# Attention with chosen chunks and a gated MLP: w_in products split for three batches, x^T copied by VectorE, a new order on every engine

## The chip, the cores and the metric

The kernel runs on one core of a Trainium2 chip. The metric is the device time of one execution in microseconds. The core's engines are named as the profile names them: PE (TensorE, with PEld for its weight loads), DVE (VectorE), ACT (ScalarE), POOL (GpSimd) and SP (SyncE, which here only issues DMAs).

## The reference

Two stages follow each other. The first is attention over 4 batches, 8 heads, 768 positions and head size 64, in which each query sees only the 6 chunks (of 32 keys) that an upper bound of its scores ranks highest. The second is a gated MLP over the result.

```python
# attention: k in 24 chunks of 32 keys
k_min, k_max = k_chunks.min(axis=3), k_chunks.max(axis=3)
ub = np.sum(np.maximum(q * k_min, q * k_max), axis=-1)      # for each query and chunk
ub = np.where(causal, ub, -1e9)
top_chunks = np.argsort(ub, axis=-1)[..., -6:]
scores = np.where(sel & causal_positions, scale * q @ k.T, -1e9)
attn = softmax(scores)
x = (attn @ v)                                              # (4, 768, 512)
# gated MLP
h = gelu_tanh(x @ w_in)                                     # (4, 768, 1024)
u, v = h[..., :512], h[..., 512:]
v_n = (v - mean) / sqrt(var + 1e-6) * g_ln
v_s = einsum('ts,bsd->btd', w_sg, v_n) + b_sg[None, :, None]
out = x + (u * v_s) @ w_out
```

## The kernel before

The work is cut into 16 **pairs** of heads (pair p holds heads 2p and 2p+1) and 4 **batches** (batch b is made of pairs 4b to 4b+3). Everything is written down as a list of operations in `_build`. Each has an engine, a function that issues its instructions, and the names of what it reads and writes; `link` turns these into semaphore waits. The order is not the order of that list. `TABLE` holds, for each engine, the numbers of its operations in the order in which it issues them, and in `slots` the PSUM slot of every tile; `place` follows it. Each engine issues strictly in its order, so an operation that waits holds up all that stand behind it on the same engine, and SP's list is one queue for nearly all DMAs.

For each pair: two loads each of k rows and q rows and one or two of v rows (`load_rows` L527, `load_v` L536 and L542, into three buffers each); fp32 transposes on PE (L549); minimum and maximum of each chunk on DVE (L577) and their difference (L596); copies of the transposed k and q out of PSUM on ACT or DVE (`evac`, L449 for ACT and L452 for DVE); the positive part of q (L615 on ACT, L618 on DVE) and a cast of q on POOL (L624); the upper bounds on PE (L659 for pairs 0 to 3, L706 for two pairs at once after that); then on DVE transposes of the bounds (L669, L715), the 8 largest of each (L676, L726), a comparison (L682, L731) and the transpose of the mask (L686, L734). From pair 4 on, DMAs bring the mask (L739), the copy of k (L590) and constant rows (L593, L751) into the operands of the scores, so that one matmul gives score and mask. The scores (L833 and L839, or L794) go through the exponential on ACT (L848, or L800), POOL zeroes the part above the diagonal (L857, L805), and PE multiplies with v (L878, and L884 on the diagonal). DVE divides by the sum (L894, L896) and writes x into `XS`.

For each batch, x must be transposed for the product with w_in. Its four quarters dk = 0 to 3 belong to the four pairs. In batch 0 all four are transposed on PE (`xtrans`, L918) and copied out of PSUM. In batches 1 to 3 the first three are transposed by a DMA (L905) and only the last on PE. The constant `XEV` names the engine of that copy, batch by batch.

`moe_h` computes h: six tiles of 128 rows for the half that is normalized (L942, then the gelu on ACT, L947, and statistics on DVE, L951), and eight tiles for u (L961, gelu L967). Each tile is a sum of four matmuls over dk. For b < `HSPL` a tile is two operations, one over dk = 0 to 2 and one over dk = 3, and its PSUM tile may lie in any of four slots; otherwise it is one operation, and in batches 0 to 2 its tile lies in slots 2 or 3:

```python
cut = NDK - 1 if b < HSPL else 0
t = ps_g.tile((2, 3) if not cut and b < B - 1 else None)
for x, (k0, k1) in enumerate(((0, cut), (cut, NDK)) if cut else ((0, NDK),)):
```

`moe_g` follows: the normalized half (L995, after a power on POOL, L983) times w_sg (L1013), scaled and shifted on DVE (L1030), times u (L1034), times w_out (L1046), plus x (L1055, into `osb` or `vgb`), stored by L1062. The weights come by DMA (L441) into buffers that are free at the start, and POOL casts them (L445); w_sg is also transposed on PE (L495). Gelu and the exponential need different tables on ACT, so ACT runs all gelus of a batch in one go, with a table load before and after.

Of the kernel before, what the change touches and what calls it, by code (L numbers as in the profile page):

```python
# [10 lines left out]
F32 = mybir.dt.float32  # L11
# [249 lines left out]
def _build(nc, ctx, q, k, v, w_in, g_ln, w_sg, b_sg, w_out, out):  # L261
# [4 lines left out]
    NT = S // 128  # L266
# [22 lines left out]
    def T(name, shape, dt):  # L289
        return ctx.enter_context(nc.sbuf_tensor(name, list(shape), dt))  # L290
# [18 lines left out]
    NQS = 3  # L309
    NBULK = 0  # L310
# [15 lines left out]
    HSPL = 1  # L326
# [18 lines left out]
    XEV = ("act","act","act","act")  # L345
    qn = [T(f"qn{i}", [128, NT, 2, DH], F32) for i in range(NQS)]
    kn = [T(f"kn{i}", [128, NT, 2, DH], F32) for i in range(NQS)]
# [174 lines left out]
    def load_rows(p, nm, src, dst):  # L522
        s = p % NQS
        for h0, h1 in ((0, 1), (1, 2)) if p < SPLIT else ((0, 2),):
            for i in range(2):
                j0, j1 = 3 * h0, 3 * h1
                P.op("act" if i == 1 and p < BOTH else "sp", lambda e, i=i, j0=j0, j1=j1: e.dma_start(  # L527
                    dst[s][:, j0:j1, i, :], bass.AP(src.tensor, (2 * p + i) * S * DH + 128 * DH * j0,
                                                    [[DH, 128], [128 * DH, j1 - j0], [1, DH]])), dmac(),
                     (nm, p, i, h0), writes=[(nm, s, h, i) for h in range(h0, h1)], dma=f"{nm}{s}_{i}{h0}",  # L530
                     xfer=XROW * (h1 - h0) / 2, bulk=NBULK)

# [21 lines left out]
    def kside(p):  # L554
        s, w = p % NQS, p % NW
# [555 lines left out]
    for p in range(4, NP + 4):  # L1111
# [39 lines left out]
    "act": (  # L1151
# [11 lines left out]
    "dve": (  # L1163
# [18 lines left out]
    "pool": (  # L1182
# [80 lines left out]
```

## Time and profile before

| what | value |
|---|---|
| median of 3 runs | 218.98 us (217.86 to 219.22) |
| the profiled execution, time | 216.24 us |
| the profiled execution, span | 214.4 us |
| granted TensorE clock in it | 0.998 |
| PE busy | 202.5 us, 94% of the span |
| DVE busy | 184.2 us, 86% |
| ACT busy | 162.0 us, 76% |
| POOL busy | 89.0 us, 41% |
| DMA, packets' time as a share of 16 engines' span, the largest queue | 72.3% |

A row of a timeline or of the chain has the start in us from the span's start, the length in us, the engine, the line, and what is written from what; in brackets behind it stands how long the engine had been idle and what ended that. A row of the groups has busy time and mean nanoseconds of one instruction behind the bar, then the idle time before them. A row for one line has least, median and greatest duration in ns.

| stretch, us from the span's start | what PE mostly does there |
|---|---|
| 0 to 44.7 | pairs 0 to 3: transposes, bounds, scores, values |
| 44.7 to 58 | w_in products of batch 0 |
| 58 to 98.8 | w_sg and w_out of batch 0, attention of pairs 4 to 7 |
| 98.8 to 113 | w_in products of batch 1 |
| 113 to 152.5 | w_sg and w_out of batch 1, attention of pairs 8 to 12 and most of 13 |
| 152.5 to 165 | w_in products of batch 2 |
| 165 to 184.9 | w_sg and w_out of batch 2, the rest of the attention |
| 184.9 to 214.4 | batch 3's MLP and the last stores |

### The profile page before, as it was taken

To read this page: it belongs to the slowest core of one execution; us is meant where nothing else is said; L and a number is where in the kernel's file an instruction comes from. 1 tells how busy PE (TensorE), PEld (TensorE's weight loads), DVE (VectorE), ACT (ScalarE), POOL (GpSimd) and SP (SyncE) were. 2 spreads that over 40 slices of the span, in tenths; PEclk is the share of its full clock that TensorE was granted. 3 is DMA by queue.
4 is the path that set the end of the run, shared out by engine and by line. 5 is a ranking of instruction groups with operands and counts; after the bars stand their busy time and mean duration, and the time that the engine had idled before them with its cause. 6 is when DMAs were issued, how large, how long until landed. Compare 5 with 4: busy or idle time off the path is not lost.

```text
span 214.4 us, 5903 instructions
## 1 busy us (share of the span) xinstructions
PE 202.5 (94%) x2314; PEld 133.7 (62%) x2326; DVE 184.2 (86%) x534; ACT 162.0 (76%) x249; POOL 89.0 (41%) x119
## 2 busy tenths in 40 slices
PE   7979999999999899997999899999999999999993
PEld 3547777745766577785466577679545668555642
DVE  3999999779999999894999798979797876778994
ACT  2468999988599599999769988989967888664000
POOL 8426598993274357634120664565202313002000
PEclk9999999999999999999999999999999999999999
DMA  7999989997999969898998986753721006201207
GB/s 152 219 218 192 280 193 293 343 346 149 223 228 256 178 194 235 183 172 212 243 214 182 204 193 181 180 162 90 68 48 28 3 25 152 46 3 49 98 26 268
DMA packets 91338, 36.06 MB, mean 168 GB/s; under 512 B 84144, under 2 KB 86448, under 8 KB 91312
## 3 DMA queue, kind: packets, MB, share of 16 engines
q1 hardware_dynamic: 91024, 35.31, 72.3%
q8 instruction: 18, 0.29, 0.6%
q10 hardware_dynamic: 288, 0.39, 0.5%
q14 instruction: 8, 0.07, 0.1%
HBM read 24.77 MB, written 6.29 MB: 145 GB/s over the span
## 4 chain that ended last, share of the span: by engine, by line
PE 52%; DVE 21%; ACT 9%; SPq 7%; DMA 6%; issue 2%; DVEq 0%
PE PSG L1013 8%; PE PSG L961 8%; PE PSC L794 7%; PE PSG L942 6%; PE PSG L1046 6%; PE PSG L549 4%; DVE W L577 4%; ACT E L848 4%; PE PSG L878 3%; SPq L527 3%; DVE m L726 2%; PE PSG L706 2%; DVE U L715 2%; DMA out_dram<-osb 2%; ACT E L800 2%
## 5 line engine op out<-in xcount | busy, mean ns | idle before, releaser
L800 ACT ACTIVATE E<-PSC 128x1024 bf16<-128x1024 f32 (+1 forms) x72 | 63.1, 919 | 7.6 <-PE PSC L794 7.3
L794 PE MATMUL PSC<-QA,KA 128*128 128x128 bf16 (+2 forms) x336 | 37.8, 246 | 0.6 <-DMA QA<-Dt 0.5
L577 DVE TENSOR_REDUCE W<-PSG 128x12 f32<-128x384 f32 x64 | 32.4, 546 | 3.7 <-PE PSG L549 3.7
L1013 PE MATMUL PSG<-wsgT,vhat 128*128 128x384 bf16 x192 | 34.9, 326 | 0.0
L624 POOL CAST QA<-qT 64x768 bf16<-64x768 f32 (+1 forms) x28 | 23.9, 857 | 22.9 <-ACT qT L449 16.1
L805 POOL TENSOR_SCALAR_AFFINE_SELECT E<-E 128x768 bf16<-128x768 bf16 x24 | 20.7, 862 | 29.9 <-ACT E L800 29.6
L794 PEld LDWEIGHTS PSC<-QA,KA 128*128 128x128 bf16 x336 | 24.0, 98 | 8.2 <-ACT E L800 1.9
L1013 PEld LDWEIGHTS PSG<-wsgT,vhat 128*128 128x128 bf16 x192 | 17.7, 98 | 11.3 <-DVE uT L1034 0.5
L967 ACT ACTIVATE uT<-PSG 128x384 bf16<-128x384 f32 x32 | 15.5, 490 | 11.7 <-PE PSG L961 11.1
L961 PE MATMUL PSG<-xT,winb 128*128 128x384 bf16 x128 | 23.9, 326 | 0.0
L848 ACT ACTIVATE E<-PSC 128x1024 bf16<-128x1024 f32 (+3 forms) x26 | 21.4, 863 | 2.6 <-PE PSC L839 2.2
L1046 PE MATMUL PSG<-woutb,uT 128*128 128x512 bf16 (+1 forms) x92 | 21.8, 370 | 1.3 <-DMA KA<-INDF 0.5
L1030 DVE SCALAR_TENSOR_TENSOR PSG<-PSG,glnT,bsgbc 128x384 f32<-128x384 f32 x32 | 19.8, 621 | 3.0 <-PE PSG L1013 2.7
L942 PE MATMUL PSG<-winb,xT 128*128 128x512 bf16 x92 | 21.2, 379 | 0.9 <-issue 0.5
L634 POOL CAST vx<-vn 128x768 bf16<-128x768 f32 x16 | 13.3, 833 | 20.3 <-DMA vn<-in_v_dram 16.2
L449 ACT ACTIVATE KA<-PSG 128x384 bf16<-128x384 f32 (+1 forms) x38 | 18.3, 493 | 2.8 <-DVE W L577 2.7
L878 PE MATMUL PSG<-vx,E 128*128 128x65 bf16 x480 | 19.8, 194 | 0.3 <-ACT E L800 0.2
L878 PEld LDWEIGHTS PSG<-vx,E 128*128 128x128 bf16 x480 | 17.4, 98 | 2.7 <-issue 0.7
L1034 DVE TENSOR_TENSOR uT<-PSG,uT 128x384 bf16<-128x384 f32 x32 | 17.7, 554 | 0.8
L896 DVE TENSOR_TENSOR XS<-PSG,rden 128x384 bf16<-128x384 f32 x32 | 17.6, 552 | 0.8
L951 DVE BATCH_NORM_STATS2 stats<-vgb 128x6 f32<-128x512 f32 x24 | 16.1, 687 | 2.2 <-ACT vgb L947 1.9
L961 PEld LDWEIGHTS PSG<-xT,winb 128*128 128x128 bf16 x128 | 11.7, 98 | 9.4 <-ACT uT L967 1.8
(87 smaller groups left out, 332.5 us busy)
## 6 DMA issues: line engine op xcount, KB each, us to landing
kn<-in_k_dram SPq DMA_DIRECT2D x32, 192.0 KB, 4.5
qn<-in_q_dram SPq DMA_DIRECT2D x32, 192.0 KB, 4.4
vn<-in_v_dram SPq DMA_DIRECT2D x12, 384.0 KB, 5.1
out_dram<-osb SPq DMA_DIRECT2D x18, 256.0 KB, 2.3
vn<-in_v_dram SPq DMA_DIRECT2D x8, 192.0 KB, 5.7
uT<-in_moe_w_sg_dram SPq DMA_DIRECT2D x4, 384.0 KB, 5.8
vgb<-in_moe_w_in_dram SPq DMA_DIRECT2D x3, 512.0 KB, 5.3
KA<-INDF SPq DMA_DIRECT2D x12, 96.0 KB, 3.8
```

Source lines behind the costliest of these rows:

```text
L577: P.op("dve", lambda d, m=m, op=op, src=src, h0=h0, h1=h1: d.tensor_reduce(W[w][:, m, 12 * h0:12 * h1].rearrange("p (h c) -> p h c", h=h1 ...
L624: P.op("pool", lambda g, i=i, r0=r0, r1=r1: g.tensor_copy(QA[w][i or 0][r0:r1, :], qT[r][r0:r1, :]), gps(S, 250 if i == 1 else 150), ("qca ...
L794: r = e.matmul(t.ap()[:, o:o + n], KA[w][i][:, 128 * kb:128 * kb + 128], QA[w][i][:, q0:q0 + n], start=True, stop=True)
L800: P.op("act", lambda e, t=t, c0=c0, c1=c1, i=i: e.activation(E[es][:, i, c0:c1], t.ap()[:, 0:c1 - c0], ACTF.Exp, scale=SCALE), act(c1 - c0 ...
L805: P.op("pool", lambda g, ev=ev: g.affine_select(ev, ev, pattern=[[0, NT], [1, 128]], compare_op=ALU.is_ge, fill=0.0, base=0, channel_multi ...
L848: P.op("act", lambda e, t=t, c0=c0, c1=c1, n=n: e.activation(E[es][:, :, c0:c1], t.ap().rearrange("p (i x) -> p i x", i=2)[:, :, 0:n], ACT ...
L878: r = e.matmul(t.ap()[:, 65 * (qb - q0):65 * (qb - q0) + 65], E[es][:, i, at[kb, qb]:at[kb, qb] + 128], vx[w][:, kb, i, :], start=x == 0, ...
L942: r = e.matmul(t.ap()[:, 0:F], xT[s][:, dk, 128 * qt:128 * qt + 128], winb[:, dk, F:DFF], start=(dk == 0), stop=(dk == NDK - 1), skip_grou ...
L961: r = e.matmul(t.ap()[:, 0:TG], winb[:, dk, 128 * fb:128 * fb + 128], xT[s][:, dk, TG * tg:TG * tg + TG], start=(dk == 0), stop=(dk == NDK ...
L1013: r = e.matmul(t.ap()[:, 0:TG], vhat[s][:, sb, 128 * fb:128 * fb + 128], wsgT[:, sb, TG * tg:TG * tg + TG], start=(sb == 0), stop=(sb == N ...
L1030: P.op("dve", lambda d, t=t, fb=fb, tg=tg: d.scalar_tensor_tensor(t.ap()[:, 0:TG], t.ap()[:, 0:TG], glnT[:, fb:fb + 1], bsgbc[:, TG * tg:T ...
L1046: r = e.matmul(t.ap()[:, 0:n1 - n0], gT[s][:, fb, 128 * qt:128 * qt + 128], woutb[:, fb, n0:n1], start=(fb == 0), stop=(fb == NF - 1))
```

## The change

Three constants change what is computed where. `HSPL` goes from 1 to 3: in batches 1 and 2 too, each w_in tile becomes two operations. `XEV` goes to DVE for batches 1 to 3: the copy of the last quarter of x^T leaves ACT. The number of k buffers gets a name of its own, `NKS`, and stays 3. The 28 new operations shift the numbers behind them, and all lists of `TABLE` and the slots are replaced by new ones.

```diff
+    NKS = 3
...
-    HSPL = 1
+    HSPL = 3
...
-    XEV = ("act","act","act","act")
+    XEV = ("act","dve","dve","dve")
     qn = [T(f"qn{i}", [128, NT, 2, DH], F32) for i in range(NQS)]
-    kn = [T(f"kn{i}", [128, NT, 2, DH], F32) for i in range(NQS)]
+    kn = [T(f"kn{i}", [128, NT, 2, DH], F32) for i in range(NKS)]
...
     def load_rows(p, nm, src, dst):
-        s = p % NQS
+        s = p % len(dst)
...
     def kside(p):
-        s, w = p % NQS, p % NW
+        s, w = p % NKS, p % NW
...
 TABLE = {
     "pe": (
...
     "filler": (
-        "49:7 56:4 80:4 "),
+        "49:7 56:4 84:4 "),
```

The lists say little as numbers. Decoded at the places that matter here (pt = w_sg product, hv and hu = w_in products for the normalized half and for u, with 0 and 1 for the two parts of a split one; sc = a piece of scores of a pair and head; ub = bounds; pv and pvd = products with v; ktr and qtr = fp32 transposes of k and q; xtr = transpose of the last quarter of x), PE goes from one batch's attention into batch 1's w_in products like this:

```
before: ... pv 7:1, pvd 7:1, qtr 11, ktr 11, xtr 1, sc 8:1:2, sc 8:1:0, hv 1:1, ktr 10, hv 1:3, qtr 12, sc 8:1:1, hv 1:0, hv 1:2, ktr 10, hv 1:5, hv 1:4,
        hu 0:0, ub 10, hu 2:0, hu 0:1, qtr 14, hu 3:1, hu 1:1, qtr 14, hu 1:0, hu 3:0, qtr 13, hu 2:1, pt, pt, ...
after:  ... sc 7:1:1, ktr 11, qtr 12, pv 7:1, pvd 7:1, qtr 12, ktr 11, xtr 1, hv 1:4 (0,1), hv 1:5 (0,1), hv 1:1 (0), hv 1:0 (0,1), hv 1:1 (1), hv 1:3 (0,1), hv 1:2 (0,1),
        hu ..., ub 10, hu ..., sc 8:1:0, hu ..., sc 8:1:1, qtr 14, qtr 14, pt, pt, sc 9:1:1, ...
```

and into batch 2's like this:

```
before: ... pvd 12:0, xtr 2, pv 12:1, sc 13:1:0, pvd 12:1, ub 14, sc 13:1:2, hv 2:0, hv 2:1, sc 13:0:2, sc 13:0:1, hv 2:2, hv 2:4, hv 2:3, hv 2:5, hu ...
after:  ... pvd 12:0, ub 14, sc 13:1:2, sc 13:1:0, pv 12:1, pvd 12:1, sc 13:1:1, xtr 2, sc 13:0:2, hv 2:1 (0,1), hv 2:0 (0), hv 2:3 (0,1), hv 2:0 (1), ...
```

On DVE, the copy of batch 2's last quarter stands behind the three transposes of the bounds of pairs 14 and 15 and the first search for their 8 largest. Near the start, DVE's list has the mask transpose of pair 0 (L686) before the difference of pair 1 (L596), where it had them the other way round. On SP, the first half of pair 12's k rows goes ahead of the last DMA transpose of batch 1, where it stood behind the v loads of pairs 8 and 13 and a mask of pair 9; the v rows of pair 9 go behind those of pairs 11 and 13. On POOL, a cast of q of pair 5 goes between the casts of the first and the second quarter of w_in.

More of the change, by code (lines that the diff above doesn't have):

```diff
@@ L1133 @@
     "pe": (
[17 rows of a table removed]
-    "act": (
[11 rows of a table removed]
-    "dve": (
[18 rows of a table removed]
-    "pool": (
[13 rows of a table removed]
[18 rows of a table added]
+    "act": (
[11 rows of a table added]
+    "dve": (
[18 rows of a table added]
+    "pool": (
[13 rows of a table added]
     "slots": (
-        "1032102322312301101013101101000112230100100101123102232110100023100001001102310011001320133223130222"
-        "2333223332231011003200011100103211111010010132111000111032001101133222333232232323322233222330010013"
-        "2100001010123101010101011220010010001331110100232233223233232332233223323310101023110011220000012310"
-        "011123001302123120120201021031312310"),
+        "1032230313213321000110132201001103210310101100132103232011010032101111010013210000112301322221130323"
+        "2322332232320101013300110011013211101010010023110011010023000001101022332301221223222233332231101003"
+        "2011110101023011001110100330101100101220010100133012011232003222332232323210101032111100231001002311"
+        "001033130110320131020220321311033012"),
     "filler": (
-        "49:7 56:4 80:4 "),
+        "49:7 56:4 84:4 "),
 }
```

117 rows, old and new, of the table TABLE are left out of this document.

## The prediction

> **What bounds the kernel now.** I read the page first (busy shares), then busy time by stretches cut at the w_in products, then the chain that ended last, and last the timelines around the chain's waits.
>
> ```profile
> span 214.4 us, 5903 instructions
> ...
> PE 202.5 (94%) x2314; PEld 133.7 (62%) x2326; DVE 184.2 (86%) x534; ACT 162.0 (76%) x249; POOL 89.0 (41%) x119
> ...
> PE 52%; DVE 21%; ACT 9%; SPq 7%; DMA 6%; issue 2%; DVEq 0%
> ```
> ```profile
> 0.00:44.70 44.70, 40.61 (x647) 27.80 (x648) 37.63 (x124) 34.94 (x56) 30.03 (x50) 1.00 1.06 241
> 44.70:98.80 54.10, 52.12 (x580) 35.92 (x580) 50.78 (x158) 46.36 (x75) 28.85 (x35) 1.00 0.95 208
> 98.80:112.30 13.50, 13.18 (x105) 7.84 (x107) 11.22 (x37) 10.50 (x20) 3.03 (x3) 1.00 1.03 236
> 112.30:153.40 41.10, 39.58 (x535) 29.24 (x538) 35.53 (x101) 37.56 (x53) 19.81 (x24) 1.00 0.70 164
> 153.40:165.00 11.60, 11.29 (x74) 5.19 (x73) 10.64 (x41) 8.42 (x16) 1.61 (x2) 1.00 0.41 44
> 165.00:183.40 18.40, 18.19 (x235) 13.01 (x232) 13.72 (x28) 14.65 (x17) 4.31 (x5) 1.00 0.25 57
> 183.40:214.40 31.00, 27.49 (x155) 14.72 (x156) 24.65 (x50) 9.60 (x16) 1.32 (x1) 0.98 0.24 82
> ```
>
> Columns of the second: stretch, its length, busy time of PE, PEld, DVE, ACT, POOL, the granted clock, the DMA share and GB/s. PE is idle 11.9 us in all (214.4 - 202.5), 4.1 of them before 44.7 and 3.5 after 183.4. The clock is full, so there is nothing to win there. The DMA engines are full (0.95 to 1.06) up to 112 us: a transfer that is issued a little late lands several us late, and no order can move more bytes. The matmuls are the same before and after, so the change can only win or lose waits, and I price it wait by wait. Second to PE is ACT, which from 112.3 to 153.4 is busy 37.56 of 41.10.
>
> **The start, part of the new order.** Decoded, the new DVE list puts the transpose of pair 0's mask (L686) ahead of the small subtraction of pair 1 (L596).
>
> ```profile
> 12.26 0.46 DVE Dn L682
> 12.72 0.72 DVE W L596
> 13.44 0.40 DVE Dt L686
> ```
> ```profile
> 12.29 1.11 POOL L624 CAST QA<-qT 128x768 bf16<-128x768 f32 x1 [2.50 <-ACT qT L449]
> ```
> ```profile
> L596 DVE TENSOR_TENSOR W<-W x16: 157/176/804, 7.8 to 150.5; 128x24 f32<-128x24 f32 x16
> ```
> ```profile
> L734 DVE STREAM_TRANSPOSE Dt<-Dn x6: 745/770/778, 49.6 to 160.8; 128x576 bf16<-128x576 bf16 x6
> ```
>
> The subtraction takes 0.176 us at the median and 0.804 at most; the long one lies on the chain and ends as POOL's cast does (12.29 + 1.11 = 13.40). The mask transposes never stretch (745 to 778 ns). So the transpose can start 0.72 us earlier, and the scores and the exponentials wait for it. The Trainium skill, SBUF — State Buffer, section SBUF: two separate sides, calls the port pair of VectorE and GpSimd an exclusive lock, taken against a GpSimd op by a VectorE op with two SBUF inputs, which the subtraction has and the transpose has not; this trace agrees, by the 804 against 778 ns. By that rule the sum has -0.72 here; if the transpose waited for the cast as well it would have 0. I take -0.6, with the bounds 0 and -0.72: behind it the casts of w_in on POOL, into which a query cast is now put between the first and the second, can hold the first w_in product and give some back.
>
> **The join of batch 1** (last quarter of x^T, then w_in).
>
> ```profile
> 96.06 0.49 PE L549 MATMUL PSG<-identF,kn 128*128 128x128 f32 x3
> 96.90 0.49 PE L918 MATMUL PSG<-identB,XS 128*128 128x128 bf16 x6 [0.34 <-ACT qT L449]
> 97.85 0.89 PE L794 MATMUL PSC<-QA,KA 128*128 128x256 bf16 x10 [0.46 <-DMA QA<-Dt]
> 99.12 0.81 PE L942 MATMUL PSG<-winb,xT 128*128 128x512 bf16 x3 [0.38 <-issue]
> ```
> ```profile
> 97.43 0.81 ACT L449 ACTIVATE xT<-PSG 128x768 bf16<-128x768 bf16 x1
> ```
> ```profile
> L452 DVE COPY wsgT<-PSG x6: 525/546/557, 27.7 to 55.8; 128x768 bf16<-128x768 bf16 x6
> ```
> ```profile
> 100.30 1.02 DVE L577 TENSOR_REDUCE W<-PSG 128x12 f32<-128x384 f32 x2 [2.42 <-PE PSG L549]
> ```
>
> Three idle pieces: 0.34 before the transpose, 0.46 before scores that wait for mask rows by DMA, 0.38 before the first product, 1.18 in all. In the new list the scores of pair 8 are gone from here (one into the u products, the others behind them), and behind the transpose stand the first three quarters of a product, which need only the DMA-transposed part. The copy of the last quarter goes from ACT (0.81) to DVE, where the same shape takes 0.546, into a stretch in which DVE sat idle for 2.42. I take -0.8: the 0.46 and the 0.38 go, the 0.34 stays, as the same two fp32 transposes cover the same wait. Bounds: 0, if the DMA transpose of the third quarter lands late and then stalls the split product as it stalled the whole one, to -1.18. At the same place the value products of pair 7 now follow the last scores by only two transposes, less than the exponential between them (919 ns, row below): +0.3, bounds 0 to +0.6.
>
> **Two late transfers.**
>
> ```profile
> 117.30 3.48 DMA kn<-in_k_dram
> ...
> 135.79 4.67 DMA out_dram<-osb
> ```
> ```profile
> 120.83 0.55 PE L549 MATMUL PSG<-identF,kn 128*128 128x128 f32 x3 [0.89 <-DMA kn<-in_k_dram]
> ```
> ```profile
> 141.31 1.04 PE L1046 MATMUL PSG<-woutb,uT 128*128 128x512 bf16 x4 [0.42 <-DVE osb L1055]
> ```
>
> PE waits 0.89 for pair 12's k rows and 0.42 for an output buffer whose store landed late. In SP's new list the first half of those rows is issued ahead of the last DMA transpose of batch 1, not behind the value loads of pairs 8 and 13 and a mask copy, on which SP stood; and the store of the first output tile of batch 1 now stands further ahead of the tile that reuses its buffer. I take -1.1 (bounds 0 and -1.31). What is late next in the same queue: the values of pair 9, now loaded behind those of 11 and 13. Their cast stands ahead of the value load of pair 12, which holds up SP, and with it the masks of pair 9's first head; the scores that read those masks come only after seven w_sg products, so I price it at 0 and leave the doubt to the second rival.
>
> **The w_in products of batch 2, and PSUM.** With the split, the tiles of these products may lie in any of four PSUM slots; unsplit, in batches 1 and 2, in two.
>
> ```profile
> 155.40 3.63 PE PSG L942 x16
> 159.02 0.65 PE PSG L961 x4
> 159.71 5.04 PE PSG L961 x28
> ...
> 185.15 5.13 PE PSG L942 x23
> ...
> 191.14 3.90 PE PSG L961 x24
> ```
> ```profile
>   ACT vgb L947: 3.0, 9
>   ACT uT L967: 1.8, 6
> ```
> ```profile
> 150.12 0.81 ACT L449 ACTIVATE xT<-PSG 128x768 bf16<-128x768 bf16 x1
> ...
> 153.45 1.28 ACT L947 ACT_TABLE_LOAD   x1
> ```
>
> Batch 3, which already has four slots, is the yardstick: its u products take 3.90/24 = 0.163 us a matmul, those of batch 2 5.04/28 = 0.180; times 32 that is 0.56. The v products: 3.63/16 = 0.227 against 5.13/24 = 0.214 (one record is missing), times 24 is 0.3. The two rows on x^T's readers say what PE waited for: ACT's emptying of the tiles. With four slots PE runs on through the table load of 1.28, behind which the first emptying waits, and ACT loses the copy of 0.81 ahead of it. Sum 0.86; I take -0.8 (bounds 0 and -1.1, with 0.27 that stood before the third product). Splitting itself costs no more matmuls; two issues for one I price at 0 up to +0.05 for each of 28. DVE's copy now stands behind three mask transposes and a search: it is covered by one piece of scores and the first three quarters of one product, no more; without that cover it costs its 0.55.
>
> **The join of batch 3** is not split; only the copy changes engine.
>
> ```profile
> 185.15 1.03 PE L942 MATMUL PSG<-winb,xT 128*128 128x512 bf16 x4 [0.15 <-issue]
> ```
>
> 0.15 idle there; the copy is 0.81 - 0.546 = 0.26 shorter: -0.1 (0 to -0.26; DVE's next instruction is behind it and waits for PE, +0.3 at worst).
>
> **Sum.** -0.6 - 0.8 + 0.3 - 1.1 - 0.8 - 0.1 = -3.1. The rest of the order is redrawn as well: of PE's 11.9 idle us the pieces named are 1.18 + 1.31 + 0.42, and I let the new order bring one new wait of the size of a named one against each two that go: +0.6, bounds -1 and +3. Net -2.5: span 211.9, the profiled execution from 216.24 to 213.7. The median of the runs, 218.98, is 2.74 above that execution; with the same difference the forecast is **216.5 us**.
>
> **Rivals.** *All of it comes true and nothing comes back*: the bounds added, -0.72 - 1.18 - 1.31 - 1.1 - 0.26 = -4.6, gives 214.4. For it: the waits have other names and no common cause. Against: DMA is full to 112 us, so someone always waits.
>
> *Given back*: the gains are eaten by new waits for transfers, at +3 for the redrawn order: about 219. For it: SP's list is changed nearly everywhere, and the row at 117.30 shows that one late transfer costs most of a microsecond; against: the loads that stalled PE are issued earlier.
>
> *Slower, ACT becomes the bound between the w_in products of batches 1 and 2.*
>
> ```profile
> L800 ACT ACTIVATE E<-PSC 128x1024 bf16<-128x1024 f32 (+1 forms) x32 | 28.2, 919 | 3.0 <-PE PSC L794 2.9
> ...
> L615 ACT ACTIVATE rT<-qT 128x576 f32<-128x576 f32 x4 | 2.7, 683 | 0.1
> L449 ACT ACTIVATE qT<-PSG 128x384 f32<-128x384 f32 x5 | 2.4, 492 | 0.3 <-PE PSG L549 0.3
> ```
>
> In that stretch the new list has 35 exponentials, not 32 (+3 x 0.88 = 2.6 by 28.2/32), two more query copies (+1.0), one relu less (-0.7) and no x^T copy (-0.8): +2.1. ACT would be busy 39.7 of 41.1, with 1.4 to spare against 3.5 now. From the point where its idle time stays above 1.4 it decides. With the idle time of now it costs 2.1; if the scores come too late behind pairs of w_sg products and it doubles, 5.6. In the middle, 3.9, with the start's -0.6 kept and the rest lost: 222.3. Against: PE has work moved into the same stretch (the other scores of pair 8 and three query transposes, out of the w_in products of batch 1, which get shorter), so that ACT's load comes with time to bear it.
>
> *The change doesn't do what it says*: the third buffer constant is 3 in both, so no buffer is gained; the split and the copies are in the new lists (28 more products on PE, three copies moved). No chance is given to it.
>
> **How the numbers follow.** Forecast 0.47, all of it true 0.08, given back 0.20, ACT bound 0.25. Some 1% (2.2 us) is what a measurement of this kernel can tell from no change. Of the forecast's case 0.36 lies beyond -1% and 0.11 within; all of it true is beyond; given back is 0.18 within and 0.02 slower; ACT bound is 0.02 within and 0.23 slower. Faster 0.44, same 0.31, slower 0.25. The forecast's own range is 215.0 to 218.0; to hold 8 in 10 it reaches from 213.5 over "given back" into the slower rival at 221.5.
>
> **What would show it.** Right: the mask transpose L686 at about 12.7 and the first masked scores before 13.4; behind the transpose L918 of batches 1 and 2 a product L942 with under 0.2 idle; no idle for pair 12's k rows; the u products of batch 2 at 0.165 us a matmul; three copies of x^T on DVE at 0.55. Wrong: ACT busy 39 or more from the end of batch 1's products to the start of batch 2's and PE waiting for E there (the slower rival); PE idle in many pieces behind DMA landings (given back); the start unmoved at 44.7, with the products waiting for POOL's casts of w_in.

## The result and the profile after

| kernel | median us | least to greatest | runs | ratio of runs to before, 95% interval |
|---|---|---|---|---|
| before, beside after | 217.86 | 215.43 to 220.26 | 17 | |
| after | 215.54 | 215.37 to 216.02 | 17 | 0.9928 [0.9904, 0.9952] |

The kernel became faster (by 0.7% by the ratio, 1.1% by the medians), and its spread fell from 4.8 us to 0.65 us. The ratio leaves out runs of before that lie more than 1.5% above its fastest one, so it shows less than the medians (215.54/217.86 = 0.989). The two profiled executions lie closer still: 216.24 and 215.41 us, spans of 214.4 and 213.3. So two questions follow: where 1.1 us of span went, and where the rest of the 2.3 us between the medians comes from.

The page of after (busy shares), and its busy time by stages, cut near where the w_in products begin and end (columns as in the prediction):

```profile
span 213.3 us, 5898 instructions
...
PE 202.3 (95%) x2312; PEld 133.1 (62%) x2326; DVE 186.3 (87%) x537; ACT 158.8 (74%) x246; POOL 88.7 (42%) x119
```
```profile
0.00:47.05 47.05, 41.34 (x648) 27.29 (x648) 40.63 (x127) 35.48 (x57) 30.97 (x52) 1.00 1.08 248
47.05:100.60 53.55, 52.05 (x575) 35.89 (x580) 50.13 (x156) 46.45 (x77) 28.70 (x35) 1.00 1.01 208
100.60:112.90 12.30, 12.24 (x99) 6.14 (x98) 10.19 (x26) 8.34 (x16) 3.00 (x3) 1.00 1.00 204
112.90:153.20 40.30, 40.09 (x548) 30.27 (x551) 37.11 (x121) 37.56 (x54) 19.31 (x24) 1.00 0.74 168
153.20:164.90 11.70, 11.65 (x84) 6.51 (x84) 10.15 (x33) 9.41 (x18) 1.96 (x2) 1.00 0.14 30
164.90:182.60 17.70, 17.58 (x216) 12.33 (x216) 14.21 (x29) 14.07 (x15) 3.45 (x4) 1.00 0.27 41
182.60:213.30 30.70, 27.37 (x154) 14.62 (x154) 23.92 (x49) 7.50 (x14) 1.32 (x1) 0.99 0.25 93
```

PE's work did not change, so I compare its idle time (length minus PE's column), stage by stage, before and after: 4.09 to 5.71 at the start, 1.98 to 1.50, 0.32 to 0.06, 1.52 to 0.21, 0.31 to 0.05, 0.21 to 0.12, 3.51 to 3.33. The start lost 1.6 us, and everything behind it won 2.6, both against this one execution of before. Two things stay hidden in such a comparison: a stall between two products that still overlap leaves no idle time, and another execution of before has other waits. Both matter below.

The start of after, from the timelines of ACT, PE and PEld (weight loads):

```profile
46.18 1.51 ACT L450 ACTIVATE xT<-PSG 128x768 bf16<-128x768 bf16 x2 [0.58 <-PE PSG L919]
```
```profile
10.16 0.69 PE L660 MATMUL PSG<-qT,W 64*32 64x288 f32 x8 [1.07 <-ACT CMb L431]
...
27.05 0.40 PE L834 MATMUL PSC<-QA,KA 64*128 64x384 bf16 x4 [0.57 <-DVE Dt L687]
...
44.49 0.72 PE L707 MATMUL PSG<-qT,W 64*32 64x288 f32 x16 [0.48 <-DVE XS L897]
```
```profile
47.06 0.34 PEld L943 LDWEIGHTS PSG<-winb,xT 128*128 128x128 bf16 x3 [0.76 <-DVE U L716]
```

The first U product waits 1.07 for ACT's copy of a constant, which stands behind two key copies and two q copies in ACT's list. The first w_in product waits 0.76: its last operand is the first of the two copies at 46.18 (0.8 us of the 1.51), whose transpose PE issues only behind a U product. (The releaser that the row names is not the late one; the matmul's own record is missing, so its weight load is shown.)

The joins and the late transfers, PE and DVE of after:

```profile
100.36 0.49 PE L919 MATMUL PSG<-identB,XS 128*128 128x128 bf16 x6 [0.28 <-ACT qT L450]
100.91 3.37 PE L943 MATMUL PSG<-winb,xT 128*128 128x512 bf16 x14
...
122.73 0.49 PE L550 MATMUL PSG<-identF,kn 128*128 128x128 f32 x3
...
142.39 1.03 PE L1047 MATMUL PSG<-woutb,uT 128*128 128x512 bf16 x4
...
153.51 5.13 PE L943 MATMUL PSG<-winb,xT 128*128 128x512 bf16 x23
158.47 3.09 PE L962 MATMUL PSG<-xT,winb 128*128 128x384 bf16 x18
...
161.83 2.44 PE L962 MATMUL PSG<-xT,winb 128*128 128x384 bf16 x14
```
```profile
100.89 0.56 DVE L453 COPY xT<-PSG 128x768 bf16<-128x768 bf16 x1 [0.22 <-PE PSG L919]
```

The products of batch 1 follow the transpose without a wait, while DVE's copy of 0.56 runs beside the first three quarters. Pair 12's key transpose (122.73) and the w_out products of batch 1 have no bracket any more.

### The profile page after: what moved, and what is told of

It reads as the page before. It is cut to its first block, busy times and chain, and to the rows that moved or that the text cites. A ratio compares the mean times of both kernels' runs of the same rounds, so it can differ in the third digit from the quotient of the medians.

```text
span 213.3 us, 5898 instructions
## 1 busy us (share of the span) xinstructions
PE 202.3 (95%) x2312; PEld 133.1 (62%) x2326; DVE 186.3 (87%) x537; ACT 158.8 (74%) x246; POOL 88.7 (42%) x119
## 4 chain that ended last, share of the span: by engine, by line
PE 72%; DVE 14%; ACT 9%; issue 2%; POOL 1%; DVEq 0%; POOLq 0%
PE PSG L1014 15%; PE PSC L795 11%; PE PSG L962 10%; PE PSG L943 10%; PE PSG L1047 9%; PE PSG L550 5%; PE PSG L879 5%; ACT E L801 5%; DVE W L578 4%; PE PSG L707 3%; PE PSG L885 2%; ACT E L849 2%; ACT KA L450 1%; DVE XS L897 1%; DVE m L677 1%
## 5 line engine op out<-in xcount | busy, mean ns | idle before, releaser
L962 PE MATMUL PSG<-xT,winb 128*128 128x384 bf16 x128 | 22.9, 326 | 0.0
L968 ACT ACTIVATE uT<-PSG 128x384 bf16<-128x384 f32 x32 | 14.7, 490 | 10.9 <-PE PSG L962 10.7
L948 ACT ACTIVATE vgb<-PSG 128x512 f32<-128x512 f32 x24 | 13.3, 598 | 6.4 <-PE PSG L943 6.4
```

What stands on the lines that cost most here:

```text
L962: r = e.matmul(t.ap()[:, 0:TG], winb[:, dk, 128 * fb:128 * fb + 128], xT[s][:, dk, TG * tg:TG * tg + TG], start=(dk == 0), stop=(dk == NDK ...
```

## The experiments

At first two theories stood against each other. A spread is the greatest less the least time of a kernel's runs. **S**: the gain and the narrow spread come from transfers that land with time to spare in the new lists. **P**: they come from the split products and the DVE copies. Each median below is to be read against before in the same comparison: 217.73 for the first four, 218.24 for e5 to e8, 217.89 for e9 to e11, 217.90 for e12.

**e1, no split**, in after's order:

```diff
-    HSPL = 3
+    HSPL = 1      # whole products where the second part stood
```

Only the split goes. The tiles stay in the slots that after's list gives them, which for batches 1 and 2 are all four; before's list uses two.

> The changed kernel with its own new order, but the w_in products of batches 1 and 2 whole again, each where its second part stood. Theory S (the gain comes from transfers that land with time to spare in the new lists): 215.5 to 216.2 us, at most 0.6 above the changed kernel, and as narrow a spread of its runs (under 1 us). Theory P (the gain comes from the split products and the copies on DVE): the products wait again for the last quarter of x^T, 0.4 to 0.8 us in each of two batches and more in the emptying of their tiles, 216.5 to 217.5 us.

Measured: 216.81 us (216.38 to 217.29, one far outlier of 412 aside), ratio 0.9989 [0.9959, 1.0018]: 1.27 above after and by the ratio not to be told from before, the spread still narrow.

```profile
101.72 5.35 PE L943 MATMUL PSG<-winb,xT 128*128 128x512 bf16 x24 [0.65 <-DVE xT L453]
...
154.72 5.38 PE L943 MATMUL PSG<-winb,xT 128*128 128x512 bf16 x24 [0.38 <-DVE xT L453]
159.94 2.11 PE L962 MATMUL PSG<-xT,winb 128*128 128x384 bf16 x12
...
162.33 3.41 PE L962 MATMUL PSG<-xT,winb 128*128 128x384 bf16 x20
```

PE waits for the copy at both joins, 0.65 + 0.38 = 1.03. That is what the split covers, and the time lies in P's range.

**e2, copies back on ACT**, in after's order:

```diff
-    XEV = ("act","dve","dve","dve")
+    XEV = ("act","act","act","act")   # ahead of the first gelu (batches 1, 3) or of the last exponential (2)
```

> The changed kernel, but the three copies of the last quarter of x^T back on ACT: ahead of the first gelu in batches 1 and 3, ahead of the last exponential in batch 2. Theory S: 215.4 to 216.0 us, spread under 1 us. Theory P: each copy is 0.26 us longer and ACT reaches the table load 0.81 later, so PE waits 0.5 to 1 us in each batch, 216.5 to 218 us.

Measured: 217.07 us (216.95 to 217.66), ratio 0.9988 [0.9962, 1.0014], 1.53 above after and again narrow.

```profile
102.56 1.68 PE L943 MATMUL PSG<-winb,xT 128*128 128x512 bf16 x7 [0.92 <-ACT xT L450]
...
155.76 1.47 PE L943 MATMUL PSG<-winb,xT 128*128 128x512 bf16 x6 [0.56 <-ACT xT L450]
```

The second parts now wait for ACT, 0.92 + 0.56 = 1.48, which is nearly the whole difference. Three quarters of a product cover a copy that starts at once on DVE, not one that queues on ACT.

**e3, split and DVE copies in before's order**, copies behind the last division of their batch, the two parts of a product side by side, with both constants as in after. The tiles stay in before's two slots.

> The kernel before with its old order, but the products of batches 1 and 2 split, the two parts of each one behind the other, and the three copies on DVE directly behind the last division of their batch. Theory S: the old lists keep their late transfers, so the runs spread as before (215.5 to 220 us) and the median stays within 1 us of the kernel before. Theory P: 1 to 2 us below the kernel before, near the changed kernel.

Measured: 219.42 us (217.73 to 221.98), ratio 1.0082 [1.0039, 1.0125]: slower than before, with before's wide spread. P had expected 1 to 2 us less, S at most 1 us more or less, so both missed the median. So the two edits are worth something only inside the new lists; in the old order and slots, together, they cost. Each of e1 and e2 takes away the cover of the same copy, so 1.3 and 1.5 must not be added up: P holds for about half of the 2.6 us behind the start, with that condition. As e1 and e2 keep the narrow spread, that comes with the new lists. No run has the new lists with neither edit.

**e4, the start mended**, on after: ACT copies the two constants first; one of DVE's copies L412 goes behind the first four reductions; two operand copies L749 go behind pair 3's last division; POOL's cast of q of pair 5 goes behind the third w_in cast.

> The changed kernel with its start mended where its trace shows waits: ACT's two constant copies (L429, L431) ahead of the first k copy; one of DVE's constant copies (L412) behind the first four reductions; DVE's two copies of constant rows (L749) behind the last division of pair 3; POOL's cast of q of pair 5 behind the third cast of w_in. If the start is held by these places in the lists, the first product of w_in comes 1 to 2.3 us earlier (it starts at 47.1 in the changed kernel, 44.7 in the one before) and the time falls to 213.3 to 214.6 us. If the start is held by the load of the weights, it stays at 215.3 to 215.8 us.

Measured: 215.39 us (215.09 to 215.91), ratio 0.991 [0.9883, 0.9937]. The first w_in product came at 46.63 instead of 47.06 (by their weight loads), not 1 to 2.3 us earlier as expected, and by the first w_sg product of batch 1 only 0.12 was left (114.01 against 114.13). The time lies in the range that had been given for a start held by the load of the weights; that is not shown, as the start did move. Half a microsecond won there met the next thing that is not moved with it.

**e5 and e6, before unchanged, profiled twice more.** One execution took 217.73 us (span 215.9), the other 214.91 (span 213.1).

> The kernel before, unchanged, profiled again. Its runs spread from 215.4 to 222.3 us. Theory S: where this execution differs from the first profile (span 214.4), the difference sits in waits for transfers that land late (k rows of pair 12, mask rows of pair 8, the DMA transposes of the third quarter, stores of the output buffers), between 90 and 155 us, 1 us or more each. Theory P: all stretches are longer or shorter in proportion, with no wait that stands out.

> The same as e5_look1, a second execution: Theory S expects other waits for transfers to differ, in the same stretch of 90 to 155 us; theory P expects none to stand out.

The quick execution of before is quicker than after's 215.41. Of the 2.8 us between the two spans, 2.0 arise in two steps between 26 and 31 us. First the quick one (e6), DVE and then POOL:

```profile
25.48 0.46 DVE L682 TENSOR_TENSOR Dn<-U,m 128x288 bf16<-128x288 f32 x1
25.97 0.36 DVE L748 COPY KA<-INDF 64x768 bf16<-64x768 bf16 x1
...
27.18 0.47 DVE L618 TENSOR_SCALAR rT<-qT 128x576 f32<-128x576 f32 x1
```
```profile
26.52 0.83 POOL L445 CAST vhat<-uT 128x768 bf16<-128x768 f32 x1 [0.93 <-DMA uT<-in_moe_w_sg_dram]
```

Then the long one (e5), DVE, POOL and PE:

```profile
25.58 1.05 DVE L682 TENSOR_TENSOR Dn<-U,m 128x288 bf16<-128x288 f32 x1
26.66 0.90 DVE L748 COPY KA<-INDF 64x768 bf16<-64x768 bf16 x1
...
27.98 0.52 DVE L577 TENSOR_REDUCE W<-PSG 128x12 f32<-128x384 f32 x1
28.42 1.73 DVE L618 TENSOR_SCALAR rT<-qT 128x576 f32<-128x576 f32 x1
```
```profile
25.49 0.83 POOL L445 CAST vhat<-uT 128x768 bf16<-128x768 f32 x1 [0.18 <-DMA uT<-in_moe_w_sg_dram]
26.26 1.09 POOL L857 TENSOR_SCALAR_AFFINE_SELECT E<-E 128x768 bf16<-128x768 bf16 x1
27.30 0.94 POOL L624 CAST QA<-qT 64x768 bf16<-64x768 f32 x1
28.20 0.85 POOL L857 TENSOR_SCALAR_AFFINE_SELECT E<-E 128x768 bf16<-128x768 bf16 x1
29.01 0.83 POOL L634 CAST vx<-vn 128x768 bf16<-128x768 f32 x1
```
```profile
28.11 0.23 PE L833 MATMUL PSC<-QA,KA 64*128 64x128 bf16 x2 [1.14 <-DVE Dt L686]
...
30.67 0.69 PE L659 MATMUL PSG<-qT,W 64*32 64x288 f32 x8 [0.89 <-DVE wsgT L452]
```

In the long execution w_sg's rows land about 1 us **earlier**. POOL then runs back to back, and three DVE instructions are stretched by 0.59, 0.54 and 1.26 us; the reduction between them, which reads PSUM alone, is not. PE pays 1.14 + 0.89. So theory S is wrong for this part of the spread: earlier landing made it slower. The new theory, **L** (port lock): before loses some 2 us whenever POOL's casts meet DVE's operations here, and after is narrow because its lists fix how they meet. The second half of that is argued and not shown. After and e4 pay a part in their profiles (Dn at 25.31 takes 1.08, beside the masking at 24.40):

```profile
25.31 1.08 DVE L683 TENSOR_TENSOR Dn<-U,m 128x288 bf16<-128x288 f32 x1
```
```profile
24.40 1.68 POOL L858 TENSOR_SCALAR_AFFINE_SELECT E<-E 128x768 bf16<-128x768 bf16 x2
```

S is not gone, though. The first profile of before (span 214.4) has the quick start of e6: weight loads of the first w_in product at 44.7, of the first w_sg product of batch 1 at 112.9 and 112.8. Its 1.3 us more arise behind that, where PE waited 0.89 for pair 12's k rows and 0.42 for an output buffer. e6 has no wait for those rows and 0.2 for that buffer, so that between batch 1's and batch 2's products its PE idles for 0.22 us, the first profile's for 1.52 and after's for 0.21. Transfers that are late in one execution and not in the next are thus a second source of spread, and the first profile had caught them.

**e7, before with time given to its late transfers**: in SP's list the k rows of pair 12 earlier, the v rows of pairs 12 and 13 and the k rows of pair 14 later.

> The kernel before with only SP's list changed between 100 and 127 us: the k rows of pair 12 ahead of those of pair 13, and the v rows of pairs 12 and 13 and the k rows of pair 14, which landed 21 to 28 us before their use, behind the masks of pairs 10 and 11. Nothing is split and no copy is moved. Theory S: 1 to 2 us below the kernel before in the median, and a spread of under 3 us. Theory P: the median within 0.5 us of the kernel before, and the same spread.

Measured: 217.26 us (214.95 to 219.88), ratio 0.9925 [0.9883, 0.9966]. The wait for pair 12's k rows was gone and the median 1.0 below before, so that part of S holds; the spread of 4.9 us stayed. Its profile has the long steps of e5 (PE idles for 1.46 us between 26 and 31).

**e8, e4 with another order of the last transposes of batch 0** (quarter 0 ahead of quarter 1, its copy too), and two value loads that land over 30 us early moved back.

> e4_start with two more places mended: the transpose of the first quarter of batch 0 ahead of the second (the first w_in product waited 0.61 to 0.83 for its copy), and the v rows of pairs 13 and 14, which landed 36 and 32 us early, behind the mask copy of pair 8 and the last k rows of pair 13 in SP's list (in e4_start the start's gain of 0.43 was lost at 113 us, where PE waits for the q rows of pair 14). If these two are what held it: 214.2 to 215.0 us. If the gain is lost again at another transfer: 215.2 to 215.6 us.

Measured: 216.25 us (215.78 to 216.52), ratio 0.9911 [0.988, 0.9943]: a miss, 0.86 slower than e4.

```profile
45.16 0.84 PE L919 MATMUL PSG<-identB,XS 128*128 128x128 bf16 x12 [1.25 <-ACT xT L450]
```

PE's next two transposes wait for a copy that ACT comes to late: 1.25 us here, to save the wait ahead of the first w_in product.

**e9 and e10, before with one load moved**: the second block of w_sg's rows one place earlier, or one place later, in SP's list.

```diff
 SP: ... ws 0, qn 4:1, ws 1, kn 5:1, vn 1:1 ...
+e9:  ... ws 0, ws 1, qn 4:1, kn 5:1, vn 1:1 ...
+e10: ... ws 0, qn 4:1, kn 5:1, ws 1, vn 1:1 ...
```

> Kernel before with one load moved: the second block of w_sg's rows goes one place earlier in SP's list, straight behind the first block. New theory L (port lock): the spread of before comes from the moment at which these rows land; when they land early, GpSimd's casts run back to back from about 25.5 us and the VectorE operations between 25.5 and 30 us (Dn, KA, rT) are stretched by 2 to 2.4 us in all. Landing earlier by one load must then make the long mode the rule: Dn about 1.05 us instead of 0.46, the fourth U product at 30.5 us or later, median 218.5 to 219.5, and few runs under 217. Theory S (late transfers): a load that lands earlier costs nothing, median as before (217.7 to 218.2) or faster.

> Kernel before with the same load moved one place later, behind the next k load. L: the casts come after VectorE's Dn and KA in nearly every run, Dn 0.46 us, the fourth U product between 28.5 and 29.5 us (up to 0.9 us may go to the transpose that waits for the later rows), median 215.5 to 216.8, spread under 2.5 us where before has over 4. S: a transfer that lands later can only cost, median 218 to 219.

Measured: e9 218.19 us (216.81 to 219.59), ratio 1.0028 [0.9996, 1.006]; e10 217.03 us (216.15 to 217.87), ratio 0.9991 [0.9961, 1.0022]. Later landing is quicker than earlier landing at the median by 1.2 us and has a spread of 1.7 us, as L and against S, which expected 218 to 219 for e10. L's numbers were too bold: e9's median is 0.3 under the range and just inside S's (217.7 to 218.2), e10's 0.2 over it, and neither ratio is clear of 1. So the rows speak for L more plainly than the medians. DVE and PE of e9, then DVE and POOL of e10:

```profile
26.38 0.46 DVE L682 TENSOR_TENSOR Dn<-U,m 128x288 bf16<-128x288 f32 x1
26.87 0.90 DVE L748 COPY KA<-INDF 64x768 bf16<-64x768 bf16 x1
...
28.63 1.73 DVE L618 TENSOR_SCALAR rT<-qT 128x576 f32<-128x576 f32 x1
```
```profile
30.88 0.69 PE L659 MATMUL PSG<-qT,W 64*32 64x288 f32 x8 [0.89 <-DVE wsgT L452]
```
```profile
27.10 0.44 DVE L618 TENSOR_SCALAR rT<-qT 128x576 f32<-128x576 f32 x1
```
```profile
27.14 1.09 POOL L445 CAST vhat<-uT 128x768 bf16<-128x768 f32 x1 [1.74 <-DMA uT<-in_moe_w_sg_dram]
```

In e9 two of the three are stretched (Dn came too late for it, which L had not expected), in e10 none: there POOL's cast is the one that waits (1.09 for 0.83).

**e11, after mended by L**: e4, and

```diff
 POOL: ... cast of q 3, masking 1:0,
-      masking 1:1, w_sg cast 0, cast of q 4 (2nd), w_sg cast 1, v cast 1,
+      cast of q 4 (2nd), masking 1:1, v cast 1, w_sg cast 1, w_sg cast 0,
       cast of q 4 (1st) ...
 DVE:  the subtraction L597 and rT L619 of pair 3 straight behind the mask transpose of pair 2
 ACT:  the second copy of q of pair 4 straight behind the first
 SP:   v loads of pairs 13 and 14 later
```

> Kernel after with the start mended as in e4_start, and GpSimd's work at 24 to 32 us put in another order (only one masking operation ahead of VectorE's Dn, then the cast of q of pair 4, which cannot start before 27 us, then the rest), VectorE's subtraction and scaling for the fourth U product straight behind the mask transpose, and two value loads that land over 30 us early put behind the q rows of pairs 13 and 14. L: Dn 0.46 us instead of 1.08, subtraction 0.2 us instead of 0.75, the fourth U product about 1.0 us earlier than in e4_start (29.0 instead of 30.0), the first w_in product at 45.8 to 46.2 (46.63), no q-row wait at 113 us, median 214.4 to 215.0. S: only the two value loads matter, 215.1 to 215.4 as e4_start, the fourth U product unmoved.

Measured: **214.25 us** (214.12 to 214.68), ratio 0.9854 [0.9821, 0.9888], with a span of 212.5 in its profile. That is 1.3 us under after, and each of its 6 runs is quicker than the quickest one seen of before (214.91). DVE and POOL:

```profile
25.35 0.46 DVE L683 TENSOR_TENSOR Dn<-U,m 128x288 bf16<-128x288 f32 x1
```
```profile
24.45 0.87 POOL L858 TENSOR_SCALAR_AFFINE_SELECT E<-E 128x768 bf16<-128x768 bf16 x1
25.50 1.00 POOL L625 CAST QA<-qT 64x768 bf16<-64x768 f32 x1 [0.18 <-ACT qT L450]
```

POOL is idle for 0.18 just when Dn starts, Dn takes 0.46, and now the cast is the stretched one. The fourth U product came at 29.30 (e4: 30.00; expected 29.0), the first w_in product at 46.21. This time the gain lasted: the first w_sg product of batch 1 came at 113.29 (after: 114.13), and the rest ran 0.8 earlier than in after. That points to the q rows of pair 14 as what had stopped e4, since the value loads moved back stood ahead of them; no run separates it from the other edits.

**e12, before with both**, the moves of e7 and that of e10.

> Kernel before (whole w_in products, x^T copies on ScalarE, its own lists) with two moves in SP's list: the second block of w_sg's rows one load later (as e10_late) and the k rows of pair 12 ahead of loads with time to spare (as e7_spare). If before's time is its plain sequence plus two separate mishaps, the port lock at 25 to 30 us and late transfers at 98 to 127 us, both go: fourth U product at 28.4 us, no step at the transpose of pair 12's keys, median 215.3 to 216.2 and a spread under 1.8 us; kernel after would then be worth no more than 0 to 0.7 us against a mended before. If the mishaps are not separate (one only moves to the other), it stays at 216.8 to 217.3 as either move alone gave.

Measured: 217.58 us (215.90 to 220.19), ratio 0.9995 [0.9957, 1.0033]. This missed: the spread was back. DVE and POOL of its profiled execution:

```profile
22.07 1.03 DVE L618 TENSOR_SCALAR rT<-qT 128x576 f32<-128x576 f32 x1
...
24.02 1.13 DVE L416 TENSOR_TENSOR INDF<-IND 128x768 bf16<-128x768 bf16 x1
...
28.71 1.05 DVE L618 TENSOR_SCALAR rT<-qT 128x576 f32<-128x576 f32 x1
```
```profile
23.92 0.83 POOL L445 CAST vhat<-uT 128x768 bf16<-128x768 f32 x1 [1.13 <-DMA uT<-in_moe_w_sg_dram]
```

DVE is stretched as L says, but at other instructions: this execution was 0.5 us late already at its first U product (9.59 against 9.11 in e6), and with casts that start when a DMA lands, DVE met them elsewhere. PE's waits for an output buffer (0.7) and for mask rows (0.4) stood in it too. So the rows of e5, e6, e9, e10 and e11 show the stretching and what it costs PE at 25 to 31 us, but one load's place does not cure it, and how much of the spread it makes stays open. What varies in the first 8 us from run to run was not tried.

## Why the prediction was right, and where only the sum was

The time was forecast as 216.5, 1.0 above the measured median, and 215.54 lies inside the range. Its steps fared less evenly.

- **Start, -0.6: the step was right, the stage was not.** The mask transpose follows Dn directly (12.87, 13.36), and PE's largest wait there fell from 1.4 to 0.6; between 10 and 15 us its idle time fell from 1.40 to 0.87. But the first U product came at 10.16 instead of 9.21, so the first masked scores stand at 13.90, where before had them at 13.88 and the forecast before 13.4: nothing was won in time. PE's idle time grew by 0.8 before 10 us (the constant's copy), by 0.4 between 25 and 35 us (Dn) and by 0.8 behind 40 us (divisions, copy of quarter 0): +1.6 for the stage. I had priced the one reversal that I saw in the lists and left the rest to a lump of +0.6 for the redrawn order. That lump is the term that failed: 1.6 + 0.53 = 2.2 of new waits stand in the start alone.
- **Join of batch 1, -0.8 and +0.3.** Up to the end of batch 1's products behind the start, idle time fell by 0.48 + 0.26 = 0.74. As forecast, the waits for mask rows and for the product went and the one before the transpose stayed (0.34 to 0.28). e1 and e2 show that this needs both edits.
- **Late transfers, -1.1.** Idle time from 113 to 153 us fell by 1.31, which is 0.89 + 0.42. e7 shows a gain from moved loads alone (1.0 at the median). But e6, unchanged, has hardly any of these waits: from the first w_sg product of batch 1 to the end the first profile took 101.4 us, e5 100.8, e6 100.2, and after 99.2. So that the full 1.31 was there to be won is luck with the profiled execution.
- **PSUM slots, -0.8: the sum fits, and its parts only half.** PE's idle time there fell by 0.26; that is the wait of 0.27 ahead of the third product, which the sum had left out. The rest hides in PE's busy time. A row ends with its last product's own 0.326 us, so the step from product to product is the length less 0.326, over one product less: (3.09 - 0.326)/17 = 0.163 us and (2.44 - 0.326)/13 = 0.163 for the u products of after, against 0.180 before (one row of 5.90 us for 32). That is 0.55 over 32, as forecast from batch 3. The v products won nothing: their step is 0.217 in before and in e1, and the 0.3 came of dividing rows with such a tail by 16 and by 24. The step goes with the slots and not with the split: e1, whole products in four slots, has 0.162, and e3, split products in two slots, has 0.180 and the wait of 0.27. The runs with before's slots have 0.180 (e5, e6, e7, e9, e10 and e12 too), those with after's 0.163 or a little less (e2, e4 and e11 too). The order changes with the slots, and no run changes the slots alone.
- **Join of batch 3, -0.1.** Idle time fell by 0.09 + 0.18 in the last two stages.
- **The sum.** The terms behind the start sum to -2.5, and PE's idle time there fell by 2.6 against the one execution from which they were priced. The start turned -0.6 + 0.6 into +1.6. The span should have been 211.9 and was 213.3.
- **The median.** I carried before's difference of 2.74 between median and profile over to after. After has a difference of only 0.13. That the median fits so well is luck, as two errors cancel: the start was 1.6 us worse than forecast, and the spread, which I had taken as given, disappeared; 215.41 + 2.74 would have been 218.15. Of the 2.3 us between the medians of one comparison, 0.83 is between the profiled executions (216.24 - 215.41) and 1.49 is spread (217.86 - 216.24 against 215.54 - 215.41). With e6 as before's profile the first part would be -0.5: the change makes the kernel steadier more than it makes its best execution quicker.
- **The rivals.** ACT as the bound did not come: ACT has 37.56 of 40.30 busy between the two batches' products, PE idles for 0.21 there. "Given back" was right for the start alone, and the price was not transfers.

The Trainium skill, SBUF — State Buffer, section SBUF: two separate sides, says that the pair of ports is locked for a whole instruction and that the loser is blocked until it ends. The rows of e5 agree with that: Dn and KA end late beside POOL's work, and the reduction, which reads PSUM alone, stays at 0.52. They go further for rT, which by its times waited through the end of one POOL instruction and all of the next (28.42 to 29.84).

## What to carry to other kernels

Compare idle time stage by stage, and where products follow each other without a gap, the steps from start to start as well. When an order is replaced, price every stage of it, not the reversals that catch the eye. A spread of runs is itself a cost with a place: profile the same kernel several times and compare a quick with a long execution before taking the difference between profile and median as fixed, or a wait in one profile as there to be won. Moving work off an engine or splitting it paid here only with an order that lets other work run meanwhile; in the old order and slots, the same two edits made this kernel slower.

## What was unexpected of the hardware

In e5 against e6, a transfer that landed about 1 us earlier went with 2 us more on PE: GpSimd's casts, started by the landing, then ran without gaps beside VectorE, and a scaling of 0.45 us took 1.73, a copy of 0.36 took 0.90. The order in which the two engines arrive decides which of them pays: in e10 and e11 it was GpSimd's cast (1.09 and 1.00 for 0.83). That was cheaper, but not free in e10, where PE waited 0.4 for a later cast of GpSimd.
